# Later chunks' last two values products moved between the fourth up quarter and its rest, and a new order of the steps

## The chip, the cores and the metric

The kernel runs on one core of one Trainium2 chip. The metric is the device time in microseconds of one execution; a time is the median of the runs shown. The profile is of one execution, whose own time stands beside its span.

## The reference

Two blocks follow one another. An mLSTM cell (batch 4, 8 heads, 768 steps, head size 40) is followed by a dense layer pair with an exact gelu (3072 tokens, 320 to 2048 to 320), all in float32:

```python
for t in range(S):
    m_new = np.maximum(f_gate[:, :, t] + m, i_gate[:, :, t])
    f_stab = np.exp(f_gate[:, :, t] + m - m_new)
    i_stab = np.exp(i_gate[:, :, t] - m_new)
    C = f_stab[..., None, None] * C + i_stab[..., None, None] * np.einsum('bhd,bhe->bhde', vt, kt)
    n = f_stab[:, :, None] * n + i_stab[:, :, None] * kt
    h_tilde = np.einsum('bhde,bhe->bhd', C, qt)
    denom = np.maximum(np.abs(np.einsum('bhd,bhd->bh', n, qt)[:, :, None]), 1.0)
    y[:, :, t] = o * h_tilde / denom          # o = sigmoid(o_gate)
x = y.transpose(0, 2, 1, 3).reshape(B * S, H * D)
h = x @ w_in
out = (0.5 * h * (1.0 + erf(h / sqrt(2)))) @ w_out
```

## The kernel before

**Chunks.** The 768 steps are cut into six chunks of 128. Within a chunk the cell is written as matrix products: decayed scores of q and k (tile `W`), their product with the values (`values`, `later_values`, tile `ph`), and the part that comes from the state carried in from earlier chunks (`read_two`, tile `pf`, scaled into the tile `far`). The sum of the last two is `hs`. `finish` divides it and applies the output gate, `turn_y` transposes the result into `px`, and `split_x` makes the operands of the dense layers of it.

**Dense layers.** Each chunk has 512 tokens (4 batches of 128). Every float32 operand is split into parts of fewer bits, and three products of parts stand for one (`x_hi`, `x_rest`, `x_low`; `g_parts`; `w_out_part`). The up product is made in four quarters: `up` (line 966: 24 products with 128 rows, tile `pu`) and then `up_rest` (line 977: 12 with 64 rows). `gelu` (lines 984 to 987) takes a bank of it to `g_whole` and three parts. `down` (line 991) adds 12 products of one row block into the accumulators `po`, one bank for each batch. A bank has 512 columns and `po` uses 320; the view `beside` names 164 columns behind them.

**The order is written by hand.** Three strings of words give the order in which the steps are issued: `FRONT` for chunk 0, all gates, the weights' conversion and the cell of chunk 1; `SECOND` for the dense layers of chunk 1 beside the cell of chunk 2; `LATER` for those of chunks 2 to 4 beside the cells of 3 to 5. `LAST` (chunk 5, dense layers alone) does not change. `play` calls the step of each word. Each engine, and each queue, executes what it is given in that order; between engines there are waits on data and buffers only.

**Letters of the later chunks** (the number is the quarter, the batch or the row block): `U`/`u` up and up_rest, `g` gelu, `d` down, `E` finish of the chunk before (output copy, line 1015, and its sends, line 859, on SP's queue), `L` load of the blocks of q and k, `K`/`Q` their transposes (line 512, VectorE), `D` weighing of the values (line 539, GpSimd), `C` read_two (line 621), `h` update_two (lines 632 to 647), `S` scores_two (lines 568, 574), `V` later_values (lines 674, 678), `Y` the cell's finish (lines 685 to 690), `t` twice (line 699, ScalarE), `X` turn_y (lines 708, 718), `R` split_x (lines 727, 728), `M` mask (line 474, GpSimd), `W` exponentials (line 500), `G` gate (line 506), `B`, `J`, `O` loads, `+` one copy from DRAM to DRAM. A number of 4 or more means the next chunk's cell.

**Letters of the front** that the argument uses: `K` conv_one (lines 404, 405, ScalarE) and `J` conv_two (lines 416, 419, VectorE) convert piece after piece of the weights (tiles `sig` and `pow`, two buffers each; `J` also issues a later piece's load); `z` splits a row block of chunk 0's gelu (873, 875 on ScalarE, 874 on VectorE); `a`/`b` split rows of w_out (935, 943); `F` is one row block of chunk 0's down product (line 888), sixteen in all, the last six made of parts; `X`, `Y`, `R`, `G` belong to the cell of chunk 1; `r` and `p` send the gates out and back.

**Buffers the change touches.** The pool `outp` has two buffers with the tag `o_sb`, which hold the output until it is sent; `raw` has two with the tag `sig`, used for `g_whole` in the later chunks; `fars[0]` has two with the tag `hs`. `side` and `main` are two pairs of PSUM pools, two banks under each tag, that change places from chunk to chunk. In `later_values` the batches 0 and 1 write `beside` without starting a new sum and the batches 2 and 3 a bank of their own.

Of the kernel before, what the change touches and what calls it, by code (L numbers as in the profile page):

```python
# [9 lines left out]
F32 = mybir.dt.float32  # L10
# [4 lines left out]
OP = mybir.AluOpType  # L15

P = 128
# [6 lines left out]


FRONT = """
    O0 L0 k1 P0 E L1 L2 t0 P1 k7 K w0 g0 N s0 w1 O1 O3 D k4 t1 P2 w2 c0 v0 J y0 Q s1 L3 O2 K d w3 q t2 L4 P3 v1
    g1 c1 J y1 s2 K x0 t3 x1 v2 g2 O4 J B4 g3 c2 y2 s3 B5 K x2 K L5 J T0 K v3 A y3 M1 x3 c3 G0 M0 H O7 O6 O5 J
    J i5 u0 L6 u1 K W0 J W1 I4 A K S0 T1 C0 J i6 V0 i7 u2 G2 K U M2 L7 S1 J G1 K U i8 W2 J i9 C1 T2 K
    M3 f2 S2 V1 Y0 T3 J Y1 C2 e W3 K K K J S3 J C3 f3 K X0 J K R0 J K J V2 K Y2 J J K  # L30
    K V3 X1 J K r F J K (0 )0 F J K F K J F X2 G3 F J K F Y3 R1 J K F p + + + + J F J a10,2 b10,2 z10 a12 b12 F X3 z11 F a13,3 b13,3 z12 F z13 [1 F B8 z14 F B9 R2 z15 F R3 B10 B11 F a8 b8 a9 b9 F"""
CELL = "MWGVYXRKQDCSht"

HI_AT = {3: ("w_out3", 0), 8: ("w_out3", 2), 4: ("w_out0", 0), 5: ("w_out0", 1), 6: ("w_out2", 0), 7: ("w_out2", 1), 9: ("f0", 0)}
# [1 line left out]
for at, first, key in ((HI_AT, 10, "h0"), (LO_AT, 10, "h1"), (HI_AT, 13, "b0"), (LO_AT, 13, "b1"), (HI_AT, 0, "b2"), (LO_AT, 0, "b3")):  # L36
    at.update((first + i, (key, i)) for i in range(3))
LATER = """
 U0 u0 E0 E1 E2 E3 K1 Q1 L2 D0 D1 C0 h0 M2 M3 g0 g1 g2 g3 +
 U1 u1 g4 d0 g5 d1 g6 d2 g7 S0 d3 K2 Q2 L3 W2 W3 G0 G1 G2 G3 +  # L40
 U2 V0 V1 u2 g8 d4 g9 K3 Q3 B4 B5 J0 J1 d5 g10 d6 g11 S2 L4 d7
 U3 u3 + M4 M5 Y0 Y1 D2 D3 K4 W4 W5 g12 t0 d8 g13 t1 d9 g14 X0 X1 R0 d10 g15 R1 C2 h2 O0 O1 d11 V2 V3 Y2 t2 B6 J2 d12 Y3 t3 Q4 L5 B7 d13 X2 X3 R2 d14 R3 d15 + O2 O3"""

SECOND = """
 U0 u0 j2 o0 o1 K1 Q1 L2 M0 M1 D0 D1 W0 W1 a0,3 b0,3 a3 b3 a4,2 b4,2 a6,2 b6,2 C0 h0 M2 M3 g0 g1 g2 g3 o2 o3 + +
 U1 u1 Z Z Z g4 d0 g5 d1 g6 d2 g7 S0 d3 K2 Q2 L3 W2 W3 G0 G1 G2 G3 Z Z +
 U2 V0 V1 u2 + g8 d4 g9 K3 Q3 B4 B5 J0 J1 d5 g10 d6 g11 S2 L4 d7
 U3 u3 + M4 M5 Y0 Y1 D2 D3 K4 W4 W5 g12 t0 d8 g13 t1 d9 g14 X0 X1 R0 d10 g15 R1 C2 h2 O0 O1 d11 V2 V3 Y2 t2 B6 J2 d12 Y3 t3 Q4 L5 B7 d13 X2 X3 R2 d14 R3 d15 + O2 O3"""

LAST = """  # L50
 U0 u0 E0 E1 E2 E3 g0 g1 g2 g3 U1 u1 g4 d0 g5 d1 g6 d2 g7 d3 
# [5 lines left out]
def kernel(  # L57
# [16 lines left out]
    nc = tc.nc  # L74

    B, H, S, D = q.shape
    L = P
    NCH = S // L
    NP = H // 2
    D1 = D + 1  # L80
    DP = 64
    BH = B * H
    DM = H * D
    DFF = moe_w_in.shape[1]
    NF = DFF // P
    TG = B * L
# [13 lines left out]
    raw = ctx.enter_context(tc.tile_pool(name="raw", bufs=2))  # L100
    two = ctx.enter_context(tc.tile_pool(name="two", bufs=2))
    outp = ctx.enter_context(tc.tile_pool(name="outp", bufs=2))
    dram = ctx.enter_context(tc.tile_pool(name="dram", bufs=1, space=bass.MemoryType.DRAM))
    ps_tr = ctx.enter_context(tc.tile_pool(name="ps_tr", bufs=2, space=bass.MemoryType.PSUM))
    ps_h = ctx.enter_context(tc.tile_pool(name="ps_h", bufs=2, space=bass.MemoryType.PSUM))
    ps_mm = ctx.enter_context(tc.tile_pool(name="ps_mm", bufs=2, space=bass.MemoryType.PSUM))
# [25 lines left out]
    vb = [const.tile([P, H, D1], F32, name=f"vb{n}", tag=f"vb{n}") for n in range(NQ)]  # L132
# [63 lines left out]
    def turn_of(n):  # L196

        return n % NLD if n < 2 * B else (n - 2 * B) % NQ
# [184 lines left out]
    bits, sig, pow2 = {}, {}, {}  # L383
# [51 lines left out]
    def per_head(t, c, b):  # L435
        return t[:, c, b * H:(b + 1) * H].unsqueeze(2)
# [9 lines left out]
    def in_place(x, b):  # L446

        return x.rearrange("p k (a t) -> p (k a) t", a=2)[:, :, b * R:(b + 1) * R]
# [9 lines left out]
    class Cell:  # L458
# [153 lines left out]
        def read_two(self, b0):  # L612

            c, two_b = self.c, (b0, b0 + 1)
            banks = self.banks = [self.side[1][0].tile([P, H + NP, D1], F32, name="pf", tag=self.side[1][1]) for _ in range(2)]
            for i, b in enumerate(two_b):
                qT = self.qT[b]
                for p in range(NP):
                    for r in halves:
                        for hip in range(2):  # L620
                            nc.tensor.matmul(banks[hip][r, NP * i + p, :], qT[halves[hip], p, r],  # L621
                                             state[b][halves[hip], p, 0:D1], start=True, stop=True)

        def update_two(self, b0):

            c, two_b, banks = self.c, (b0, b0 + 1), self.banks
            if c + 1 < NCH:
                for i, b in enumerate(two_b):
                    vw = self.vw.pop(b)
                    for p in range(NP):  # L630
                        for hip in range(2):
                            nc.tensor.matmul(banks[i][used[hip], H + p, :], k_later[turn_of(c * B + b)][:, 2 * p + hip, :],  # L632
                                             vw[:, 2 * p + hip, :], start=True, stop=True)
            add = []
            for i, b in enumerate(two_b):
                self.far[b] = fars[0].tile([P, H, D1], F32, name="far", tag="hs", bufs=2)
                by_hip = lambda t, hip: t.rearrange("p (m two) d -> p m two d", two=2)[:, :, hip, :]
                for hip in range(2):
                    nc.vector.tensor_tensor(out=by_hip(self.far[b], hip), in0=banks[hip][:, NP * i:NP * i + NP, :],  # L639
                                            in1=by_hip(per_head(gT, c - 1, b), hip).to_broadcast([P, NP, D1]), op=OP.mult)  # L640
                if c + 1 < NCH:
                    st, d = state[b][:, :, 0:D1], dec[:, c - 1, b * NP:(b + 1) * NP].unsqueeze(2).to_broadcast([P, NP, D1])
                    nc.gpsimd.tensor_tensor(out=st, in0=st, in1=d, op=OP.mult)
                    for r in used:
                        add.append((st[r], banks[i][r, H:H + NP, :]))
            for st, to in add:
                nc.vector.tensor_tensor(out=st, in0=st, in1=to, op=OP.add)

# [11 lines left out]

        def later_values(self, b):

            n, hs = self.c * B + b, self.far.pop(b)
            Pm = W.pop(n)
            by_hip = lambda t: [t.rearrange("p (m two) d -> p m two d", two=2)[:, :, hip, :] for hip in range(2)]
            if b < 2:
                ph = beside[2 * b:2 * b + 2]
            else:
                whole = self.side[0][0].tile([P, H, D1], F32, name="ph", tag=self.side[0][1])
                ph = by_hip(whole)  # L670
            for hip in range(2):
                for p in range(NP):
                    for r in quarters:
                        nc.tensor.matmul(ph[hip][r, p, :], Pm[:, 2 * p + hip, r], vb[turn_of(n)][:, 2 * p + hip, :], start=b > 1,  # L674
                                         stop=True, skip_group_check=b < 2)
            self.hs[b] = hs
            for to, x in zip(by_hip(hs), ph) if b < 2 else ((hs, whole),):
                nc.vector.tensor_tensor(out=to, in0=x, in1=to, op=OP.add)

        def finish(self, b):  # L680
            n, hs = self.c * B + b, self.hs.pop(b)
# [18 lines left out]

        def turn_y(self, b):
            n, t = self.c * B + b, slice(b * L, (b + 1) * L)
            pool, tag = self.side[b // 2] if self.c > 1 else (ps_tr, "tr") if self.c > 0 else (ps_mm, "b")
            px = pool.tile([P, NX + 1, L], F32, name="px", tag=tag)
            unread(px[:, 0, :])
            for k in range(NX + 1):
                y = ob[n % NLD][:, k * P:(k + 1) * P] if k < NX else self.rest.get(b, y_rest).rearrange("p two r -> p (two r)")
                nc.tensor.transpose(px[:, k, :], y, ident)  # L708
            self.turned.append(b)
            if self.c < 2 and len(self.finished) > len(self.turned):  # L710
                self.twice(b + 1)
            if self.c == 0:
                nc.scalar.copy(out=first_x[:, :, t], in_=px)
                return
            self.px[b] = px
            if "x" not in parts:
                parts["x"] = raw.tile([P, NX + 1, TG], F32R, name="x_hi", tag="x", bufs=1)
            nc.scalar.activation(out=in_place(parts["x"], b), in_=by_set(px), func=AF.Copy, scale=PART)
            if self.c == 1 and b < 2:
                load(n + NLD, 1, 3)  # L720
# [12 lines left out]
    parts, fars, w_hi, w_lo, beside = {}, [], {}, {}, []  # L733
# [304 lines left out]
    def first_blocks():  # L1038
# [3 lines left out]
        for r in (32, 96):  # L1042
# [8 lines left out]
                 d=lambda: decays_last(0, 1), q=lambda: decays_last(1, NCH - 1), r=halves_out, p=halves_back,  # L1051
                 A=in_turn(first_up_steps(0)), U=in_turn(first_up_steps(1)), e=first_blocks, F=in_turn(first_down_steps(first_g)),
                 K=in_turn(lambda i=i: conv_one(i) for i in n_pieces), H=products_begin,
                 J=in_turn(lambda i=i: conv_two(i) for i in n_pieces), Z=split_weight,
# [53 lines left out]
```

## Time and profile before

| | us |
|---|---|
| median of 3 runs | 438.81 (438.38 to 438.86) |
| the profiled execution, own time | 438.46 |
| its span (first to last instruction) | 436.7 |
| chunk 1's dense layers | 118.85 to 184.72 of the span |
| chunk 2 / 3 / 4 | from 184.72 / 249.96 / 315.52 |
| chunk 5, end of its products | 379.39 / 433.0 |

In the rows of the profile a line has the engine (PE is TensorE, PEld its weight loads, DVE VectorE, ACT ScalarE, POOL GpSimd, SPq the queue of DMAs issued by SyncE), the line of the kernel, the operation, the tiles written and read, their shapes and a count. A timeline gives the start, the duration and, in brackets, the engine's idle time before it with what ended it. The chain of waits goes back from the last instruction, each time to what released it.

### The profile page before, as it was taken

The page shows a single profiled execution, that of the slowest core. Times are in us where ns is not written, and L with a number is a line of the kernel's source. Part 1 is how long each engine was busy: PE and PEld are TensorE (multiplying, and loading weights), DVE is VectorE, ACT ScalarE, POOL GpSimd, SP SyncE. Part 2 cuts the span into 40 slices and gives each one's busy share as a digit, 9 for nine tenths or more (in the row PEclk, how much of TensorE's full clock was granted, in tenths as well). Part 3 has the DMA queues.
Part 4 walks back from the last instruction along what each step waited for, and adds up shares of the span by engine and source line. Part 5 has one row for each costly group of instructions (what it writes and reads, how often), then busy time and mean ns, then how long its engine had stood idle before and what let it go on. Part 6 is the DMA issues. An engine that isn't in the chain of part 4 may idle for free.

```text
span 436.7 us, 13291 instructions
## 1 busy us (share of the span) xinstructions
PE 427.3 (98%) x5472; PEld 374.6 (86%) x5472; DVE 296.0 (68%) x680; ACT 277.3 (63%) x595; POOL 48.8 (11%) x77
## 2 busy tenths in 40 slices
PE   8989999999999999999999999999999999999996
PEld 7777888877988899988899988899988889979986
DVE  8797687797888697747597747597746586533330
ACT  4989999856889985228785229785247715243441
POOL 3001030000430041030041030040010000000000
PEclk9999999999999999999999999999999999999999
DMA  7999994577791592662492653571561400010001
GB/s 151 220 214 243 233 256 87 138 211 179 229 154 56 106 176 60 115 179 50 84 187 42 123 158 60 117 134 32 110 156 17 62 2 2 22 42 2 1 2 60
DMA packets 162268, 48.83 MB, mean 112 GB/s; under 512 B 147776, under 2 KB 155232, under 8 KB 162208
## 3 DMA queue, kind: packets, MB, share of 16 engines
q1 hardware_dynamic: 161888, 47.65, 50.1%
q8 instruction: 43, 0.70, 0.6%
q10 hardware_dynamic: 320, 0.33, 0.2%
q14 instruction: 17, 0.14, 0.1%
HBM read 43.84 MB, written 9.37 MB: 122 GB/s over the span
## 4 chain that ended last, share of the span: by engine, by line
PE 73%; DVE 2%; ACT 2%; DMA 1%; issue 1%; ACTq 0%
PE po L991 31%; PE pu L966 24%; PE pu L977 7%; PE ps L568 3%; PE pf L621 2%; PE ph L674 1%; PE po L888 1%; PE po L674 1%; PE px L708 1%; DMA bits<-in_moe_w_out_dram 1%; PE pf L632 1%; DVE pow L416 1%; DVE w_out L419 0%; ACT w_out_part L935 0%; ACT g_part L873 0%
## 5 line engine op out<-in xcount | busy, mean ns | idle before, releaser
L991 PE MATMUL po<-w_out_part,g_parts 128*128 128x320 f32 x960 | 140.7, 303 | 0.0
L991 PEld LDWEIGHTS po<-w_out_part,g_parts 128*128 128x128 f32 x960 | 131.6, 189 | 5.9 <-issue 4.6
L986 DVE TENSOR_TENSOR g_parts<-g_whole,g_parts 128x512 fp32r<-128x512 f32 x80 | 57.0, 713 | 58.1 <-ACT g_parts L985 56.0
L984 ACT ACTIVATE g_whole<-pu 128x512 f32<-128x512 f32 x80 | 47.1, 589 | 74.2 <-PE pu L977 63.7
L985 ACT ACTIVATE g_parts<-g_whole 128x512 fp32r<-128x512 f32 x80 | 50.5, 631 | 8.3 <-PE po L991 5.1
L474 POOL TENSOR_SCALAR_AFFINE_SELECT W<-W 128x1024 f32<-128x1024 f32 (+2 forms) x20 | 21.7, 1088 | 189.2 <-DMA W<-M_d 154.4
L500 ACT ACTIVATE W<-W,aT 128x128 f32<-128x128 f32 x128 | 38.8, 389 | 0.3
L987 DVE CAST g_parts<-g_whole 128x512 fp32r<-128x512 f32 x80 | 36.2, 453 | 0.0
L699 ACT COPY far<-ob 128x128 f32<-128x128 f32 x16 | 4.6, 290 | 32.9 <-DVE ob L690 32.9
L966 PE MATMUL pu<-x_hi,w_in_hi 128*128 128x512 f32 x80 | 24.2, 384 | 0.0
L966 PE MATMUL pu<-x_hi,hi_first 128*128 128x512 f32 x80 | 24.0, 381 | 0.1
L966 PE MATMUL pu<-x_rest,hi_first 128*128 128x512 f32 x80 | 23.8, 379 | 0.0
L966 PE MATMUL pu<-x_rest,w_in_hi 128*128 128x512 f32 x80 | 23.8, 379 | 0.0
L966 PE MATMUL pu<-x_low,w_in_lo 128*128 128x512 f32 x80 | 23.8, 379 | 0.0
L966 PE MATMUL pu<-x_low,w_in 128*128 128x512 f32 x80 | 23.8, 379 | 0.0
L888 PE MATMUL po<-w_out,g 128*128 128x320 f32 x80 | 22.0, 432 | 0.0
L404 ACT ACTIVATE sig<-bits 128x320 f32<-128x320 f32 (+1 forms) x26 | 15.2, 586 | 10.4 <-issue 6.1
L574 DVE TENSOR_TENSOR W<-ps,W 128x256 f32<-128x256 f32 (+1 forms) x48 | 17.7, 414 | 4.2 <-PE ps L568 3.2
L888 PEld LDWEIGHTS po<-w_out,g 128*128 128x128 f32 x80 | 15.0, 190 | 5.9
L639 DVE TENSOR_TENSOR far<-pf,gT 128x164 f32<-128x164 f32 x32 | 8.4, 319 | 16.1 <-PE pf L632 11.7
L416 DVE SCALAR_TENSOR_TENSOR pow<-sig,pow 128x320 uint32<-128x320 uint32 (+1 forms) x26 | 15.4, 592 | 4.3 <-ACT pow L405 4.3
L1015 ACT ACTIVATE o_sb<-po 128x320 f32<-128x320 f32 x20 | 7.5, 443 | 16.7 <-PE po L991 16.7
(196 smaller groups left out, 778.9 us busy)
## 6 DMA issues: line engine op xcount, KB each, us to landing
W<-M_d SPq DMA_DIRECT2D x16, 512.0 KB, 6.5
bits<-in_moe_w_in_dram SPq DMA_DIRECT2D x20, 256.0 KB, 4.2
bits<-in_moe_w_out_dram SPq DMA_DIRECT2D x16, 320.0 KB, 4.6
blocks<-kq_d SPq DMA_DIRECT2D x32, 128.0 KB, 3.5
ob<-in_o_gate_dram SPq DMA_DIRECT2D x24, 160.0 KB, 4.1
out_dram<-o_sb SPq DMA_DIRECT2D x36, 80.0 KB, 2.0
wide<-M_d SPq DMA_DIRECT2D x4, 512.0 KB, 4.8
kq_d<-in_k_dram SPq DMA_DIRECT2D x6, 320.0 KB, 4.6
```

The costliest lines, as they stand in the source:

```text
L416: nc.vector.scalar_tensor_tensor(out=p, in0=s, scalar=3, in1=p, op0=OP.logical_shift_left, op1=OP.bitwise_or)
L474: nc.gpsimd.affine_select(out=x, in_=x, compare_op=OP.is_ge, fill=1.0e30, base=base, pattern=[[0, H], [1, x.shape[2]]], channel_multiplier=-1)
L500: nc.scalar.activation(out=W[n][:, h, :], in_=src, func=AF.Exp, scale=-1.0, bias=aT[:, self.c, r:r + 1])
L574: nc.vector.tensor_tensor(out=w[r, :, t], in0=ps[i][hip][r, :, t], in1=w[r, :, t], op=OP.mult)
L888: nc.tensor.matmul(to, xs[k][:, b * L:(b + 1) * L], w, start=(n == 0 and k == 0), stop=(n == NF - 1 and k + 1 == len(xs)), skip_group_chec ...
L966: nc.tensor.matmul(in_pairs(pus[i][e]), w3(at[k])[n][:, e, i * P:(i + 1) * P], in_turns(x3[n][:, k, :]), start=(n == 0 and k == 0), stop=F ...
L977: nc.tensor.matmul(in_pairs(pus[i][e]), w3(r)[n][h, p % 2, i * P:(i + 1) * P], in_turns(x3[n][h, NX, :]), start=False, stop=(n == 2), skip ...
L984: nc.scalar.activation(out=whole, in_=self.pus[n // 4][n % 4 // 2][n % 2], func=AF.Gelu)
L985: nc.scalar.activation(out=hi, in_=whole, func=AF.Copy, scale=PART)
L986: nc.vector.tensor_tensor(out=rest, in0=whole, in1=hi, op=OP.subtract)
L987: nc.vector.tensor_copy(out=low, in_=whole)
L991: nc.tensor.matmul(in_pairs(self.po[t]), x[:, t * L:(t + 1) * L], in_turns(w), start=(n == 0 and k == 0), stop=(n == NF - 1 and k == 2), s ...
```

## The change

1. `later_values`: the batches 2 and 3 also use `beside`. After the batches 0 and 1 are added to their `hs`, VectorE writes zeros into the four `beside` views, and the batches 2 and 3 are summed onto them. Their result is copied into `hs` rather than added to `far`.
2. `update_two`: the `far` of batches 0 and 1 lies in an `o_sb` buffer, that of 2 and 3 in a `sig` buffer, and for 2 and 3 it is added to `hs` here.
3. `read_two` and `turn_y` exchange their PSUM pools between the two pairs of batches.
4. New orders. `LATER` and the second half of `SECOND`: `V2 V3` stand between `U3` and `u3`; `C2 h2` stand before `X0`; `X0` to `X3` stand singly. `LATER` alone: `C0` stands between `U0` and `u0`, `M3` before `D0`. `FRONT`: many steps are permuted; the words are the same.

```diff
 FRONT = """
-    g1 c1 J y1 s2 K x0 t3 x1 v2 g2 O4 J B4 g3 c2 y2 s3 B5 K x2 K L5 J T0 K v3 A y3 M1 x3 c3 G0 M0 H O7 O6 O5 J
-    J i5 u0 L6 u1 K W0 J W1 I4 A K S0 T1 C0 J i6 V0 i7 u2 G2 K U M2 L7 S1 J G1 K U i8 W2 J i9 C1 T2 K
-    M3 f2 S2 V1 Y0 T3 J Y1 C2 e W3 K K K J S3 J C3 f3 K X0 J K R0 J K J V2 K Y2 J J K
-    K V3 X1 J K r F J K (0 )0 F J K F K J F X2 G3 F J K F Y3 R1 J K F p + + + + J F J a10,2 b10,2 z10 a12 b12 F X3 z11 F a13,3 b13,3 z12 F z13 [1 F B8 z14 F B9 R2 z15 F R3 B10 B11 F a8 b8 a9 b9 F"""
+    c1 J y1 s2 K x0 t3 x1 v2 g2 c2 O4 J B4 y2 B5 s3 g3 K L5 J T0 x2 K K M1 v3 A y3 c3 M0 G0 x3 H J O6 O5 J O7 u0
+    L6 u1 K i5 W0 J W1 A K S0 C0 I4 T1 G2 J i6 u2 U i7 V0 K M2 S1 J G1 M3 L7 K U C1 i8 J W2 T2 i9 K f2 Y0 S2 V1
+    T3 J Y1 C2 K e W3 K J K S3 J C3 f3 K X0 J K J K K R0 J K V2 Y2 J J J K K V3 (0 X1 K F G3 J )0 J
+    K F J r F J F F X2 + R1 K K p F J Y3 + F + J z10 a12 K F a10,2 b10,2 J + b12 z11 F a13,3 b13,3 z12 F F X3 z13 F
+    B8 z14 F B9 R2 z15 F [1 R3 F a8 B10 B11 a9 b9 F b8"""
...
 LATER = """
- U0 u0 E0 E1 E2 E3 K1 Q1 L2 D0 D1 C0 h0 M2 M3 g0 g1 g2 g3 +
- U1 u1 g4 d0 g5 d1 g6 d2 g7 S0 d3 K2 Q2 L3 W2 W3 G0 G1 G2 G3 +
- U2 V0 V1 u2 g8 d4 g9 K3 Q3 B4 B5 J0 J1 d5 g10 d6 g11 S2 L4 d7
- U3 u3 + M4 M5 Y0 Y1 D2 D3 K4 W4 W5 g12 t0 d8 g13 t1 d9 g14 X0 X1 R0 d10 g15 R1 C2 h2 O0 O1 d11 V2 V3 Y2 t2 B6 J2 d12 Y3 t3 Q4 L5 B7 d13 X2 X3 R2 d14 R3 d15 + O2 O3"""
+ E0 U0 E1 E2 K1 Q1 E3 L2 D1 C0 M3 u0 D0 h0 g0 g1 g2 g3 M2 U1 u1 g4 + d0 d1 g5 g6 d2 g7 S0 d3 K2 Q2 L3 G2 W2 W3 G3 G1 G0
+ + U2 V0 V1 u2 d4 K3 g8 Q3 B4 B5 g9 d5 J0 J1 g10 d6 g11 S2 L4 d7 U3 M5 Y0 M4 W5 W4 t0 Y1 t1 V2 V3 K4 u3 D3 D2 g12 d8 + g13
+ d9 g14 C2 h2 X0 d10 Y2 g15 X1 t2 Y3 t3 Q4 d11 R0 R1 d12 O0 O1 X2 d13 R2 B6 J2 d14 X3 R3 L5 B7 + O2 O3 d15"""
...
         def read_two(self, b0):
-            banks = self.banks = [self.side[1][0].tile([P, H + NP, D1], F32, name="pf", tag=self.side[1][1]) for _ in range(2)]
+            pool, tag = self.side[0 if b0 else 1]
+            banks = self.banks = [pool.tile([P, H + NP, D1], F32, name="pf", tag=tag) for _ in range(2)]
...
         def update_two(self, b0):
-                self.far[b] = fars[0].tile([P, H, D1], F32, name="far", tag="hs", bufs=2)
+                self.far[b] = (raw.tile([P, TG], F32, name="far", tag="sig") if b0 else
+                               outp.tile([P, 2, DM], F32, name="far", tag="o_sb").rearrange("p two d -> p (two d)"))[:, 0:H * D1].rearrange(
+                                   "p (h d) -> p h d", d=D1)
...
+            for b in two_b if b0 else ():
+                hs = self.hs[b]
+                nc.vector.tensor_tensor(out=hs, in0=self.far.pop(b), in1=hs, op=OP.add)
             for st, to in add:
                 nc.vector.tensor_tensor(out=st, in0=st, in1=to, op=OP.add)
...
         def later_values(self, b):
-            n, hs = self.c * B + b, self.far.pop(b)
+            n = self.c * B + b
+            hs = self.hs[b] = self.far.pop(b) if b < 2 else fars[0].tile([P, H, D1], F32, name="hs", tag="hs", bufs=2)
...
+            ph = beside[b % 2 * 2:b % 2 * 2 + 2]
...
+            for to, x in zip(by_hip(hs), ph):
+                if b < 2:
+                    nc.vector.tensor_tensor(out=to, in0=x, in1=to, op=OP.add)
+                else:
+                    nc.vector.tensor_copy(out=to, in_=x)
+            if b == 1:
+                for x in beside:
+                    nc.vector.memset(x, 0.0)
...
         def turn_y(self, b):
-            pool, tag = self.side[b // 2] if self.c > 1 else (ps_tr, "tr") if self.c > 0 else (ps_mm, "b")
+            pool, tag = self.side[1 - b // 2] if self.c > 1 else (ps_tr, "tr") if self.c > 0 else (ps_mm, "b")
```

More of the change, by code (lines that the diff above doesn't have):

```diff
@@ L26 @@
 FRONT = """
-    O0 L0 k1 P0 E L1 L2 t0 P1 k7 K w0 g0 N s0 w1 O1 O3 D k4 t1 P2 w2 c0 v0 J y0 Q s1 L3 O2 K d w3 q t2 L4 P3 v1
-    g1 c1 J y1 s2 K x0 t3 x1 v2 g2 O4 J B4 g3 c2 y2 s3 B5 K x2 K L5 J T0 K v3 A y3 M1 x3 c3 G0 M0 H O7 O6 O5 J
-    J i5 u0 L6 u1 K W0 J W1 I4 A K S0 T1 C0 J i6 V0 i7 u2 G2 K U M2 L7 S1 J G1 K U i8 W2 J i9 C1 T2 K
-    M3 f2 S2 V1 Y0 T3 J Y1 C2 e W3 K K K J S3 J C3 f3 K X0 J K R0 J K J V2 K Y2 J J K
-    K V3 X1 J K r F J K (0 )0 F J K F K J F X2 G3 F J K F Y3 R1 J K F p + + + + J F J a10,2 b10,2 z10 a12 b12 F X3 z11 F a13,3 b13,3 z12 F z13 [1 F B8 z14 F B9 R2 z15 F R3 B10 B11 F a8 b8 a9 b9 F"""
+    O0 L0 k1 P0 E L1 L2 t0 P1 k7 K w0 g0 N s0 w1 O1 O3 D k4 t1 P2 w2 c0 v0 J y0 Q s1 L3 O2 K d w3 q t2 L4 P3 v1 g1
+    c1 J y1 s2 K x0 t3 x1 v2 g2 c2 O4 J B4 y2 B5 s3 g3 K L5 J T0 x2 K K M1 v3 A y3 c3 M0 G0 x3 H J O6 O5 J O7 u0
[3 more added lines that the diff above has]
+    B8 z14 F B9 R2 z15 F [1 R3 F a8 B10 B11 a9 b9 F b8"""
 CELL = "MWGVYXRKQDCSht"
@@ L38 @@
 LATER = """
- U0 u0 E0 E1 E2 E3 K1 Q1 L2 D0 D1 C0 h0 M2 M3 g0 g1 g2 g3 +
- U1 u1 g4 d0 g5 d1 g6 d2 g7 S0 d3 K2 Q2 L3 W2 W3 G0 G1 G2 G3 +
- U2 V0 V1 u2 g8 d4 g9 K3 Q3 B4 B5 J0 J1 d5 g10 d6 g11 S2 L4 d7
- U3 u3 + M4 M5 Y0 Y1 D2 D3 K4 W4 W5 g12 t0 d8 g13 t1 d9 g14 X0 X1 R0 d10 g15 R1 C2 h2 O0 O1 d11 V2 V3 Y2 t2 B6 J2 d12 Y3 t3 Q4 L5 B7 d13 X2 X3 R2 d14 R3 d15 + O2 O3"""
+ E0 U0 E1 E2 K1 Q1 E3 L2 D1 C0 M3 u0 D0 h0 g0 g1 g2 g3 M2 U1 u1 g4 + d0 d1 g5 g6 d2 g7 S0 d3 K2 Q2 L3 G2 W2 W3 G3 G1 G0
+ + U2 V0 V1 u2 d4 K3 g8 Q3 B4 B5 g9 d5 J0 J1 g10 d6 g11 S2 L4 d7 U3 M5 Y0 M4 W5 W4 t0 Y1 t1 V2 V3 K4 u3 D3 D2 g12 d8 + g13
+ d9 g14 C2 h2 X0 d10 Y2 g15 X1 t2 Y3 t3 Q4 d11 R0 R1 d12 O0 O1 X2 d13 R2 B6 J2 d14 X3 R3 L5 B7 + O2 O3 d15"""
 SECOND = """
[L45 to L48, printed above, removed]
+ U0 u0 j2 o0 o1 K1 Q1 L2 M0 M1 D0 D1 W0 W1 a0,3 b0,3 a3 b3 a4,2 b4,2 a6,2 b6,2 C0 h0 M2 M3 g0 g1 g2 g3 o2 o3 + + U1 u1 Z Z Z g4
+ d0 g5 d1 g6 d2 g7 S0 d3 K2 Q2 L3 W2 W3 G0 G1 G2 G3 Z Z + U2 V0 V1 u2 + d4 K3 g8 Q3 B4 B5 g9 d5 J0 J1 g10 d6 g11 S2 L4
+ d7 U3 M5 Y0 M4 W5 W4 t0 Y1 t1 V2 V3 K4 u3 D3 D2 g12 d8 + g13 d9 g14 C2 h2 X0 d10 Y2 g15 X1 t2 Y3 t3 Q4 d11 R0 R1 d12 O0 O1 X2
+ d13 R2 B6 J2 d14 X3 R3 L5 B7 + O2 O3 d15"""
 LAST = """
@@ L661, in later_values @@
         def later_values(self, b):
-            n, hs = self.c * B + b, self.far.pop(b)
+            n = self.c * B + b
+            hs = self.hs[b] = self.far.pop(b) if b < 2 else fars[0].tile([P, H, D1], F32, name="hs", tag="hs", bufs=2)
             Pm = W.pop(n)
             by_hip = lambda t: [t.rearrange("p (m two) d -> p m two d", two=2)[:, :, hip, :] for hip in range(2)]
[L666 to L670, printed above, removed]
+            ph = beside[b % 2 * 2:b % 2 * 2 + 2]
             for hip in range(2):
@@ L673, in later_values @@
                     for r in quarters:
[L674 to L678, printed above, removed]
+                        nc.tensor.matmul(ph[hip][r, p, :], Pm[:, 2 * p + hip, r], vb[turn_of(n)][:, 2 * p + hip, :], start=False,
+                                         stop=True, skip_group_check=True)
+            for to, x in zip(by_hip(hs), ph):
[6 more added lines that the diff above has]
+                    nc.vector.memset(x, 0.0)
         def finish(self, b):
```

## The prediction

> **What bounds the kernel now.** I read the busy shares first, then the chain of waits in order of time, then TensorE's timeline where its pieces do not join, and last the timelines of what it waits for there.
>
> ```profile
> span 436.7 us, 13291 instructions
> PE 427.3 (98%) x5472; PEld 374.6 (86%) x5472; DVE 296.0 (68%) x680; ACT 277.3 (63%) x595; POOL 48.8 (11%) x77
> ```
>
> TensorE has 9.4 us without work. So a new order can gain only what TensorE waits, or what it loses between its own steps, and it can lose any amount through a new wait. From 118.85 us on the chain of waits is TensorE's without a hole worth a line, but for one in chunk 1. Before that, the last place with waits is the end of chunk 0's down product (F11 to F16, 72 products of parts):
>
> ```profile
> 107.50 0.93 PE L888 MATMUL po<-w_out_part,g_part 128*128 128x320 f32 x4
> 108.70 3.53 PE L888 MATMUL po<-w_out_part,g_part 128*128 128x320 f32 x24 [0.27 <-DVE g_part L874]
> 112.61 6.24 PE L888 MATMUL po<-w_out_part,g_part 128*128 128x320 f32 x44 [0.38 <-DVE g_part L874]
> 118.69 0.59 PE L966 MATMUL pu<-x_hi,hi_first 128*128 128x512 f32 x2
> ```
>
> The last 44 start 0.138 us apart ((118.69 - 112.61) / 44). At that pace the first 4 would be through at 108.05 and the 24 at 112.01, so the two waits cost 0.65 and 0.60, together 1.25 us (the brackets show less, because the modelled ends overlap the wait).
>
> **Part 1, the front.** What is late there:
>
> ```profile
> 101.70 0.58 ACT L405 ACTIVATE pow<-bits,low_bits 128x320 uint32<-128x320 uint32 x1
> 105.26 0.50 ACT L404 ACTIVATE sig<-bits 128x320 f32<-128x320 f32 x1 [2.99 <-issue]
> 106.83 0.63 ACT L873 ACTIVATE g_part<-g 128x512 fp32r<-128x512 f32 x1
> 107.36 0.60 ACT L875 CAST g_part<-g 128x512 fp32r<-128x512 f32 x1
> 107.87 0.49 ACT L935 CAST w_out_part<-w_out 128x320 fp32r<-128x320 f32 x1
> 101.45 0.49 DVE L685 SCALAR_TENSOR_TENSOR ob<-ob,far 128x320 f32<-128x320 f32 x1 [0.58 <-ACT ob L506]
> 104.68 0.50 DVE L419 SCALAR_TENSOR_TENSOR w_out<-sig,pow 128x320 uint32<-128x320 uint32 x1
> 107.96 0.68 DVE L874 TENSOR_TENSOR g_part<-g,g_part 128x512 fp32r<-128x512 f32 x1
> 111.87 1.28 DVE L874 TENSOR_TENSOR g_part<-g,g_part 128x512 fp32r<-128x512 f32 x2
> ```
>
> ScalarE stands idle from 102.28 to 105.26 in front of K26. The profile names nothing, but `sig` has two buffers, and J24, which frees the one K26 needs, ends at 105.18 (104.68 + 0.50), behind Y3 and R1 on VectorE, which start at 101.45. Everything ScalarE gives TensorE at the end (a10, z10, a12, z11, a13, z12) is queued behind that idle K26. In the new order J24 comes before Y3, and z10 and a12 before K26: their 1.5 us (106.83 to 108.36) fill the hole. Even if K26 stayed at 105.26, z12 and all before it would come 1.5 us earlier on ScalarE, and the two late VectorE rows (z10's at 107.96, z12's at 111.87) would miss their dates no more: 1.5 is over 0.65 and over 0.60. X3 now follows F11, and r's two DMAs stand behind two loads of weight pieces, which come earlier for it. The other permutations leave the sums on ScalarE and VectorE before each of TensorE's steps about as they were, where TensorE has no wait to lose. I take -1.25; the bounds are 0 (another producer becomes as late) and -1.25.
>
> **Part 2, V2 and V3.** Their 128 products move; what do they cost in each place?
>
> ```profile
> 147.81 1.44 PE po L674 x118
> 175.22 1.48 PE ph L674 x120
> 176.69 0.35 issue
> 177.04 0.27 PE ph L674 x3
> 177.31 3.46 PE po L991 x24
> 181.46 3.26 PE po L991 x24
> 213.67 1.38 PE po L674 x112
> 241.02 1.51 PE ph L674 x117
> 306.59 1.50 PE ph L674 x114
> ```
>
> `po` rows are V0 V1 between U2 and u2, `ph` rows V2 V3 between two downs. 24 downs behind V3 take 3.46, behind downs 3.26: a further 0.20 for the change of form. Between an up and its rest I see no such loss. So a chunk saves 1.51 + 0.20 - 1.38 = 0.33 (chunk 2), the same in chunks 3 and 4, and 1.48 + 0.35 + 0.27 + 0.20 - 1.44 = 0.86 in chunk 1, if its hole of 0.35, unexplained, goes too. Together -1.85; bounds -0.5 (only the bare durations) and -1.85. C2 h2 before X0 instead of a down moves the 0.20, it does not remove it.
>
> VectorE gets four memsets and four copies of 164 columns and two additions of 328, and loses two additions. These touch the accumulators' banks, so d4 has to wait for the memsets and d8 for the copies:
>
> ```profile
> 149.00 1.03 DVE L678 TENSOR_TENSOR far<-po,far 128x164 f32<-128x164 f32 x4
> 150.74 5.09 PE po L991 x36
> L268 DVE MEMSET state<- 128x328 f32 x3 | 1.0, 332 | 0.1
> ```
>
> Chunk 1 is the tightest: the additions end at 150.03, d4 begins at 150.74 and reaches the fourth bank 0.41 later. A memset of twice the columns takes 332 ns; at half of that, four end at 150.7, at the full 332 ns at 151.4. I take 0; bounds 0 and 0.2 in one chunk. [...]
>
> **Part 3, a new wait.** `far` of batch 1 now takes the `o_sb` buffer from which E2 and E3 are being sent, and these sends are late on SP's queue:
>
> ```profile
> out_dram<-o_sb SPq DMA_DIRECT2D x36, 80.0 KB, 2.0
> 186.71 7.53 SPq L859 DMA_DIRECT2D out_dram<-o_sb  x8
> 252.20 8.37 SPq L859 DMA_DIRECT2D out_dram<-o_sb  x8
> 259.98 0.59 SPq L859 DMA_DIRECT2D out_dram<-o_sb  x1
> 317.18 7.15 SPq L859 DMA_DIRECT2D out_dram<-o_sb  x8
> 184.72 5.18 PE pu L966 x24
> 249.96 5.18 PE pu L966 x24
> 315.52 5.18 PE pu L966 x24
> 258.18 1.11 DVE L639 TENSOR_TENSOR far<-pf,gT 128x164 f32<-128x164 f32 x4 [5.44 <-PE pf L632]
> 259.21 1.34 DVE L647 TENSOR_TENSOR state<-state,pf 40x164 f32<-40x164 f32 x4
> 258.44 5.38 PE pu L966 x24
> ```
>
> In chunk 3 the last send is issued at 259.98 and lands 2.0 later, 12.0 after U0's start (249.96). By the same sum chunk 2's lands 10.9 and chunk 4's 10.2 after U0's start. VectorE wants the buffer 8.7 after it (258.18 + 0.5). What is queued behind: batch 1's `far` (0.5), the state's additions, whose first half (0.67) frees the first `pf` bank, then g0 to g3. U1's second half writes that bank; it begins at 258.44 + 0.2 + 12 x 0.216 = 261.2, 11.3 after U0's start (0.216 is 5.18 / 24). So U1 stands if the sends land later than 11.3 - 0.1 - 0.5 - 0.67 = 10.0. In the new tail the transpose Q4, which lets SP go on to the next loads and so to the sends, ends 0.5 earlier against U0, so I take landings at 10.4, 11.5 and 9.7: stalls of 0.4 in chunk 2, 1.5 in chunk 3, none in chunk 4, which also has no state to add. Together +1.9; bounds 0 (the sends go out at 0.6 each) and +2.9 (nothing comes earlier). Chunk 1 has no E.
>
> **Part 4, the tail.** Behind h2 VectorE now has `far`, additions, state, Y2, g15, Y3, Q4 and four R before U0 needs the last operand.
>
> ```profile
> 305.27 1.02 DVE L639 TENSOR_TENSOR far<-pf,gT 128x164 f32<-128x164 f32 x4
> 313.84 0.55 DVE L728 CAST x_low<-px 128x384 fp32r<-128x384 f32 x1
> ```
>
> Before, this stretch took 9.1 (305.27 to 314.39) and ended 1.1 before U0 at 315.52. Now it also holds g15 (1.0) and two R (1.9), less about 0.1 for the additions and the pauses: some 12 us. TensorE has from h2's middle to U0 11.65 us (X's 4 x 0.33, 0.20, six downs at 1.63, 0.35 of h2), and reaches the last x_low 0.86 later: 12.5. A margin of 0.5 to 0.8; I take 0.
>
> **The sum.** 438.46 - 1.25 - 1.85 + 1.9 = 437.26 against the profiled execution's own time, which is 0.35 under the median; against the median 437.61. I forecast 437.4.
>
> **The rivals.**
>
> Sends early. SP reaches them early enough, part 3 costs nothing: 437.4 - 1.9 = 435.5. For it: a send takes only 0.59 once they run. Against: in three chunks eight of them took 7.15 to 8.37.
>
> No gain in the front. Another wait takes the place of K26's: 437.4 + 1.25 = 438.65, no change. Against: the 1.5 us that z10 and a12 move.
>
> Sends later, the slower side. O3, just ahead of the sends on SP, waits for X3, which now comes 1.6 before U0 instead of 3.3. If the sends land 1.5 later than I take them, U1 stands 1.9, 3.0 and about 1 us: 4 us more, 441.4. It is slower than before from 0.8 us of lateness in each chunk, less than the spread between the three chunks now (10.2 to 12.0).
>
> VectorE the bound of the tail. If its operations stretch beside GpSimd's, U0 waits in four chunks for what exceeds the margin of part 4; at 1 us over, 4 us: 441.4 as well. Slower from 0.55 over.
>
> **How the numbers follow.** Forecast 0.42, sends early 0.20, front without gain 0.14, sends later 0.16, tail 0.08. Forecasting alone, 436.2 to 438.6. About 0.2% (0.9 us) is what can be told from no change: faster means under 437.9, slower over 439.7. Faster: most of the forecast's share (0.35) and the early sends (0.20), 0.55. Same: the rest of the forecast and the front without gain, with a little from the late cases, 0.22. Slower 0.23. The range for 8 in 10 leaves out the ends of both sides: 435.0 to 440.8.
>
> **What would show it.** F11 to F16 without a bracket, K26's idle time under 1 us, and U0 of chunk 1 near 117.6; V2 V3 at 1.4 with no dearer down behind; in chunks 2 and 3 VectorE idle before the second half of line 639 with a DMA `out_dram<-o_sb` as what ended it, and a hole in U1's middle (0.4, 1.5), none in chunk 4; no hole at U0. Wrong would be a hole at X1, d4, S0 or U0, or a U1 without one.

## The result: 0.5% slower, and the profile after

The changed kernel takes 439.96 us (median of 17 runs, 438.93 to 443.19), the kernel before, run beside it, 438.36 (17 runs, 436.52 to 440.08). The ratio is 1.0048, with a 95% interval of 1.0032 to 1.0064. The forecast was 437.4, with a range of 435.0 to 440.8. The time lies inside the range, but on the other side of the old one. The profiled execution took 440.24 us. Four of the 17 runs have a mean granted clock of TensorE of 0.995 or 0.996 and take 441.90 to 443.19 us; none of them left a trace, and the other 13 have a median of 439.64.

In the rows of the changed kernel the line numbers have moved: up is 974 (966 before), down 999 (991), the products of parts in the front 896 (888), `far` 642 (639), the state's additions 653 (647), the sends 867 (859). The experiments shift them by a few more.

The page of the changed kernel (its span, then busy time, share of the span and instructions of each engine):

```profile
span 438.5 us, 13282 instructions
PE 426.6 (97%) x5472; PEld 374.4 (85%) x5472; DVE 302.6 (69%) x712; ACT 278.6 (64%) x595; POOL 49.0 (11%) x77
```

TensorE's busy time fell by 0.7 us and the span grew by 1.8, so TensorE now waits 2.5 us longer. The chain of waits shows in which chunk. Here are the starts of U0 in chunks 1 to 5 and of U3 (225.57, 291.76, 357.05) in chunks 2 to 4:

```profile
118.45 5.18 PE pu L974 x24
...
183.52 5.18 PE pu L974 x24
...
225.57 5.18 PE pu L974 x24
...
250.20 5.18 PE pu L974 x24
...
291.76 5.18 PE pu L974 x24
...
316.38 5.18 PE pu L974 x24
...
357.05 5.18 PE pu L974 x24
...
381.17 5.18 PE pu L974 x24
```

The same view of the kernel before, U3 in chunks 2 to 4 and the last U0:

```profile
224.96 5.18 PE pu L966 x24
...
290.29 5.42 PE pu L966 x24
...
355.01 5.18 PE pu L966 x24
...
379.39 5.18 PE pu L966 x24
```

From U0 to U0 the chunks took 65.87, 65.24, 65.56 and 63.87 us before, and 65.07, 66.68, 66.18 and 64.79 after. From U3 to the next U0, where V2 V3 were moved, chunks 2 to 4 took 25.00, 25.23 and 24.38, and now 24.63, 24.62 and 24.12. What is left over belongs to the first part of each chunk:

| term | forecast | profiled execution | from |
|---|---|---|---|
| front, up to U0 of chunk 1 | -1.25 | -0.40 | 118.45 - 118.85 |
| chunk 1 and the tails of 2 to 4 | -1.85 | -2.04 | -0.80 - 0.37 - 0.61 - 0.26 |
| U0 to U3 of chunks 2 to 4 | +1.9 | +4.22 | (1.44 + 0.37) + (0.62 + 0.61) + (0.92 + 0.26) |
| sum | -1.2 | +1.78 | 440.24 - 438.46 |

The third line is the loss. TensorE's timeline around the middle of U1 in chunks 2, 3 and 4:

```profile
194.20 0.59 PE L974 MATMUL pu<-x_low,w_in_lo 128*128 128x512 f32 x2
196.37 0.67 PE L974 MATMUL pu<-x_hi,w_in_hi 128*128 128x512 f32 x2 [1.58 <-DVE state L653]
...
260.88 0.59 PE L974 MATMUL pu<-x_low,w_in_lo 128*128 128x512 f32 x2
262.48 0.67 PE L974 MATMUL pu<-x_hi,w_in_hi 128*128 128x512 f32 x2 [1.01 <-DVE state L653]
...
326.32 0.59 PE L974 MATMUL pu<-x_low,w_in_lo 128*128 128x512 f32 x2
327.79 0.67 PE L974 MATMUL pu<-x_hi,w_in_hi 128*128 128x512 f32 x2 [0.87 <-DVE far L642]
```

The products start 0.216 apart, so the second halves were due at 194.63, 261.31 and 326.75. They started 1.74, 1.17 and 1.04 us later, 3.95 together. VectorE's timeline says what it waited for in front of the second half of `far`:

```profile
195.09 0.56 DVE L642 TENSOR_TENSOR far<-pf,gT 128x164 f32<-128x164 f32 x2 [1.55 <-DMA out_dram<-o_sb]
...
261.20 0.56 DVE L642 TENSOR_TENSOR far<-pf,gT 128x164 f32<-128x164 f32 x2 [2.01 <-DMA out_dram<-o_sb]
...
327.31 0.56 DVE L642 TENSOR_TENSOR far<-pf,gT 128x164 f32<-128x164 f32 x2 [2.33 <-DMA out_dram<-o_sb]
```

This is the wait of the prediction's part 3, at the place it named, but in three chunks and not in two, and twice as long. The last sends stand in the chain (start and time until landing):

```profile
193.02 1.96 DMA out_dram<-o_sb
...
259.12 1.96 DMA out_dram<-o_sb
...
324.89 1.95 DMA out_dram<-o_sb
```

They land at 194.98, 261.08 and 326.84, which is 11.5, 10.9 and 10.5 us after U0. TensorE goes on 1.39, 1.40 and 0.95 later.

In the front the two waits are gone. TensorE's timeline of the 72 products has no bracket, and K26 stands on ScalarE without idle time behind z10 and a12:

```profile
107.94 2.03 PE L896 MATMUL po<-w_out_part,g_part 128*128 128x320 f32 x12
...
110.06 8.40 PE L896 MATMUL po<-w_out_part,g_part 128*128 128x320 f32 x60
```

```profile
102.03 0.48 ACT L943 CAST w_out_part<-w_out 128x320 fp32r<-128x320 f32 x1
102.42 0.49 ACT L404 ACTIVATE sig<-bits 128x320 f32<-128x320 f32 x1
```

Two questions remain. Is the wait for the sends the whole loss of the later chunks, and why did the front bring 0.40 where its waits were worth 1.25?

### The profile page after: what moved, and what is told of

Read it like the earlier page. It is cut to its first block, busy times and chain, and to the rows that moved or that the text cites. A ratio compares the mean times of both kernels' runs of the same rounds, so it can differ in the third digit from the quotient of the medians.

```text
span 438.5 us, 13282 instructions
## 1 busy us (share of the span) xinstructions
PE 426.6 (97%) x5472; PEld 374.4 (85%) x5472; DVE 302.6 (69%) x712; ACT 278.6 (64%) x595; POOL 49.0 (11%) x77
## 4 chain that ended last, share of the span: by engine, by line
PE 82%; issue 10%; ACT 3%; DMA 1%; DVE 1%; POOL 1%; SPq 0%; DVEq 0%; POOLq 0%
PE po L999 30%; PE pu L974 22%; PE po L896 7%; PE pu L985 6%; PE ps L568 3%; PE po L677 3%; PE pu L795 2%; PE pf L622 2%; PE px L716 2%; DMA out_dram<-o_sb 1%; ACT W L500 1%; PE pu L826 1%; ACT g_whole L992 1%; PE ps L552 1%; PE pu L801 1%
## 5 line engine op out<-in xcount | busy, mean ns | idle before, releaser
L994 DVE TENSOR_TENSOR g_parts<-g_whole,g_parts 128x512 fp32r<-128x512 f32 x80 | 55.4, 693 | 45.3 <-ACT g_parts L993 43.1
L995 DVE CAST g_parts<-g_whole 128x512 fp32r<-128x512 f32 x80 | 33.6, 420 | 0.0
L726 ACT ACTIVATE x_hi<-px 128x384 fp32r<-128x384 f32 x20 | 9.8, 488 | 21.0 <-PE px L716 21.0
L974 PEld LDWEIGHTS pu<-x_hi,w_in_hi 128*128 128x128 f32 x80 | 14.2, 189 | 6.8 <-issue 5.2
```

The lines of the kernel that those rows point to most:

```text
L974: nc.tensor.matmul(in_pairs(pus[i][e]), w3(at[k])[n][:, e, i * P:(i + 1) * P], in_turns(x3[n][:, k, :]), start=(n == 0 and k == 0), stop=F ...
L994: nc.vector.tensor_tensor(out=rest, in0=whole, in1=hi, op=OP.subtract)
L995: nc.vector.tensor_copy(out=low, in_=whole)
```

## The experiments

Ten kernels were run. Each was timed beside the kernel before (17 to 20 runs of it, medians 438.49 to 438.74) and ran 6 to 12 times; "profiled" is the one execution that left a trace.

**Both `far` in one buffer.** The changed kernel, with `far` of batches 0 and 1 side by side in one `o_sb` buffer, so that they no longer need the buffer from which E2 and E3 are sent.

```diff
-  self.far[b] = (raw.tile([P, TG], F32, name="far", tag="sig") if b0 else
-                 outp.tile([P, 2, DM], F32, name="far", tag="o_sb") ...
+  if not i and not b0:
+      both = outp.tile([P, 2 * H * D1], F32, name="far", tag="o_sb")
+  self.far[b] = (raw.tile([P, TG], F32, name="far", tag="sig")[:, 0:H * D1] if b0 else
+                 both[:, i * H * D1:(i + 1) * H * D1]).rearrange("p (h d) -> p h d", d=D1)
```

> The changed kernel, with `far` of batches 0 and 1 side by side in one `o_sb` buffer (328 columns each), so that VectorE waits for the sends of E0 and E1 alone and no longer for those of E2 and E3. Theory A (the wait of `far` for the last sends is the whole loss of the later chunks: holes of 1.74, 1.17 and 1.04 us in U1 of chunks 2, 3 and 4): the holes go, at most 0.2 us of each is left, and the profiled execution comes to 440.24 - 3.95 = about 436.3, 0.5% under the kernel before. Rival B (U1's second half has a second wait just behind, the additions of the state or the masks on GpSimd): the holes shrink to 0.5 to 1 us each and the time is 437.5 to 439. Rival C (the holes only move to the next place of the chunk): still about 440.

Measured: 436.63 us (6 runs), ratio 0.9948 (0.9932 to 0.9965), profiled 436.50. Theory A holds: this one edit turns the loss into a gain. VectorE's and TensorE's timelines show what is left, in chunk 2 alone:

```profile
193.30 1.03 DVE L643 TENSOR_TENSOR far<-pf,gT 128x164 f32<-128x164 f32 x4 [6.88 <-ACT g_parts L994]
```

```profile
194.26 0.59 PE L975 MATMUL pu<-x_low,w_in_lo 128*128 128x512 f32 x2
195.05 0.67 PE L975 MATMUL pu<-x_hi,w_in_hi 128*128 128x512 f32 x2 [0.20 <-DVE state L654]
```

`far` now runs in one piece, and U1's second half comes 0.36 late (195.05 - 194.26 - 0.43). The bracket names ScalarE; the chain leads from `far` back to a send that lands at 193.01, so what is left is a shorter wait for the sends.

**The buffer alone.** The kernel before, with only this of the change:

```diff
-  self.far[b] = fars[0].tile([P, H, D1], F32, name="far", tag="hs", bufs=2)
+  self.far[b] = (fars[0].tile([P, H, D1], F32, name="far", tag="hs", bufs=2) if b0 else
+                 outp.tile([P, 2, DM], F32, name="far", tag="o_sb") ...
```

> The kernel before, with one thing of the change alone: `far` of batches 0 and 1 in the `o_sb` ring; order, V2 V3 and front are those of before. Theory A: the last sends land 10.9, 12.0 and 10.2 us after U0 in chunks 2, 3 and 4, and U1's second half stands for what exceeds 9.9, 9.9 and 9.6: holes of 1.0, 2.1 and 0.6, together 3.7, so about 442.1, 0.8% over the kernel before. If the holes come from the new order of the sends and of the tail instead: under 439.2.

Measured: 444.38 us, ratio 1.0129 (1.0106 to 1.0152). The buffer by itself makes a hole of 1.76 us in chunk 2 and one of 2.53 in chunk 3, counted from the date at which the next product was due. TensorE's timeline in chunk 3:

```profile
261.91 0.59 PE L968 MATMUL pu<-x_low,w_in_lo 128*128 128x512 f32 x2
264.87 0.67 PE L968 MATMUL pu<-x_hi,w_in_hi 128*128 128x512 f32 x2 [2.36 <-DVE state L649]
```

Neither the order nor the place of V2 V3 is needed for the loss. Chunk 4 has no hole here, where 0.6 was expected. The time is 2.3 over the expectation, and the stretches around chunk 3's hole show most of it (busy time of each engine, then TensorE's granted clock, of which 1.00 is full speed, the DMA engines' share and GB/s):

```profile
262.00:264.80 2.80, 0.51 (x3) 0.10 (x1) 1.16 (x5) 0.00 (x0) 0.36 (x1) 1.00 0.60 114
264.80:268.80 4.00, 3.93 (x11) 3.21 (x12) 3.51 (x8) 2.17 (x4) 0.00 (x0) 0.59 0.76 132
```

Behind the hole TensorE has a granted clock of 0.59 for 4 us; by estimate that costs another 1.6 us (0.41 of 4).

**The sends first.** The changed kernel as it is, but one copy of keys and two loads of output gates stand behind the sends on SP, not ahead of them.

```diff
- E0 U0 E1 E2 K1 Q1 E3 L2 ...
+ E0 U0 E1 E2 K1 Q1 E3 + O-2 O-1 L2 ...
...
- X3 R3 L5 B7 + O2 O3 d15
+ X3 R3 L5 B7 d15
```

> The changed kernel, its buffers as they are, with one copy of keys and the two output gates' loads that stand ahead of the sends on SP moved behind them (O2 O3 of a chunk run as the next chunk's first loads). They take 1.9 us of SP's queue. If the sends follow them: landings 1.9 us earlier, 9.7, 9.1 and 8.7 us after U0, holes under 0.2 and about 436.6. If the first send's 2.6 us of waiting on SP only grows by what was moved (the queue behind it has to drain to the same date): landings and holes nearly as they are, 439.5 to 440.2.

Measured: 435.82 us, ratio 0.9938 (0.9914 to 0.9962), profiled 435.62. U1 has no hole in any chunk. The sum of the prediction without the cost of part 3, its rival "sends early", is 435.5. SP's timeline in chunk 2:

```profile
182.61 0.69 SPq L210 DMA_DIRECT2D wide<-M_d  x1
183.40 5.04 SPq L867 DMA_DIRECT2D out_dram<-o_sb  x8
188.48 0.63 SPq L182 DMA_DIRECT2D kq_d<-in_k_dram  x1
```

In the changed kernel:

```profile
185.45 8.15 SPq L867 DMA_DIRECT2D out_dram<-o_sb  x8
```

The first of these eight held SP for 2.6 us. Now they take 5.04 together, the first one no longer waits on SP, and they are through 5.4 us after U0's start (188.44 - 183.07 on the chain) where it was 10.1 (193.60 - 183.52), so 4.7 us earlier and not 1.9. So the 2.6 us for which the first send held SP belonged to the transfers ahead of it; 1.9 was the smaller part of their price.

**Three words of the front.** The kernel before, with J24 ahead of Y3 and with z10 and a12 ahead of K26, the edit that the prediction's part 1 made responsible:

```diff
- F Y3 R1 J K F p + + + + J F J a10,2 b10,2 z10 a12 b12 F
+ F J Y3 R1 z10 a12 K F p + + + + J F J a10,2 b10,2 b12 F
```

> The kernel before, with three words of the front moved: J24 ahead of Y3, z10 and a12 ahead of K26. My recorded step: TensorE's two waits of 0.65 and 0.60 in F11 to F13 go, U0 of chunk 1 starts at 118.85 - 1.25 = 117.6, the time is about 437.2. Rival (another producer is as late): U0 at 118.4 to 118.85 and 438 to 438.5.

Measured: 436.90 us (12 runs), ratio 0.9964 (0.9953 to 0.9976). TensorE's timeline has 72 products in a row, and the chain has U0 at the forecast 117.6. That it falls so near is partly luck, as the first part of this execution happened to be as early as in the profile of before (see below):

```profile
107.43 10.18 PE L891 MATMUL po<-w_out_part,g_part 128*128 128x320 f32 x72
```

```profile
117.62 5.18 PE pu L969 x24
```

**Where the front's win went.** Two kernels: the kernel before with the whole new front, and the kernel before with its own front up to S1 and the new order from there on.

> The kernel before with the whole front of the changed kernel and nothing else of it. If the 0.79 us lost ahead of 60 us belongs to that order: W0 on ScalarE at 46.5 again (45.7 to 46.6 in four executions with the order of before), U0 of chunk 1 at 118.3, time 0.4 under the kernel before, 438.1. If it was the execution's: U0 at 117.6 and 437.2.

> The kernel before, with its own front up to S1 (55 us) and the changed kernel's order of the rest. In the changed kernel TensorE is 0.79 us late at 60 us and has won 1.19 us between there and U0 of chunk 1. If the 0.79 comes from the order of the words ahead of S1 (the masks' loads and what ScalarE has to do ahead of W0): U0 of chunk 1 at about 117.65, the time about 437.3. If the win hangs on the early lateness: U0 at 118.3 or later and 437.9 or more.

Measured: 437.83 us (0.9979, 0.9965 to 0.9994) and 437.60 (0.9976, 0.9961 to 0.9991). Both expectations missed. The new front alone had U0 at 117.21 on TensorE's timeline, and the split one, with the old order in its first part, at 118.31. The timelines of all twelve traces show why. The first product of f2 (the first row `pu<-first_x_hi,hi_first`, an up product of chunk 0) falls at 62.70 to 64.09 with the new order of the first part (six executions, mean 63.5) and at 62.94 to 64.47 with the old one (six, mean 63.4). This is the spread of executions and not the order. From there to U0 it is 55.70 and 55.36 us with the old front, and 54.51 to 54.55 in all ten executions in which z10 and a12 stand ahead of K26.

**V2 V3 back.** The kernel with both `far` in one buffer, and V2 V3 taken out of U3 and put between two downs again, just before C2; then the same with one down between them and C2.

```diff
- Y1 t1 V2 V3 K4 u3 D3 D2 g12 d8 + g13 d9 g14 C2 h2
+ Y1 t1 K4 u3 D3 D2 g12 d8 + g13 d9 g14 V2 V3 C2 h2
...
+ Y1 t1 K4 u3 D3 D2 g12 d8 V2 V3 + g13 d9 g14 C2 h2
```

> The changed kernel with both `far` in one `o_sb` buffer, and V2 V3 put back between two downs, just before C2, in the zeroed columns as they are. My recorded part 2: every chunk gets dearer by 0.33 (products 1.51 for 1.38, and 0.20 for one more change of form), four chunks 1.3 together, with chunk 1's hole of 0.35 up to 1.85: 437.8 to 438.4. Rival (the place of V2 V3 is worth nothing, the loss of the holes explains all): 436.3 to 436.8.

> As values_back, but V2 V3 one down earlier, between d8 and d9, so that 12 long products stand between their 128 short ones and the 96 of C2 and h2. In values_back TensorE stood 1.46, 1.89 and 2.06 us inside C2 or h2 with nothing that the profile names, each time until 2.3 to 2.7 us after a 16 KB load of instructions began, and its granted clock was 0.62 behind the hole of 1.89. Theory F (224 short products in a row outrun TensorE's instructions): holes under 0.6 us each, no lower clock behind them, and then the place of V2 V3 alone is left, 0.33 a chunk: 436.5 + 1.3 = 437.8, with the change of form behind V3 nearer 437.3. If the hole is C2's own (a bank or an operand that it waits for, whatever stands ahead): again over 440.

Measured: 442.46 us (ratio 1.0084, 1.0053 to 1.0114) and 439.47 (12 runs; 1.0010, 0.9992 to 1.0028), against 436.63 with V2 V3 in U3. Just before C2 they cost 5.8 us. TensorE's timeline in chunk 3, the view of the DMA queues from 299 to 304 us (its first row has 40 slices of 0.125 us), and the stretch behind:

```profile
301.32 0.90 PE L622 MATMUL pf<-state,qT 64*64 64x41 f32 x47
303.89 0.45 PE L622 MATMUL pf<-state,qT 64*64 64x41 f32 x17 [1.67 <-issue]
```

```profile
DMA  0000000000000000000040000000000000000000
...
q8 instruction: 1, 0.02, 1.2%
```

```profile
304.00:308.00 4.00, 4.00 (x61) 3.88 (x61) 3.13 (x10) 1.64 (x3) 0.46 (x1) 0.62 0.25 45
```

TensorE stops inside C2, and the profile names no engine for it. The one transfer of these 5 us is a 16 KB load of instructions that begins in the slice from 301.50 on; TensorE goes on about 2.3 us after that. With 12 long products ahead of C2 the holes are gone but for one of 0.35 in chunk 4, and no lower clock follows (behind that one 12 products of down take 1.63 us on the chain, as in the other chunks, and the execution's mean granted clock is 0.999, against 0.991 with V2 V3 just before C2). So theory F stands as far as these runs go, though the time misses its 437.8. The rest of the price is mostly in the tails, 0.35, 0.63, 0.73 and 0.6 us dearer than with V2 V3 in U3, and not 0.33 each: 2.3 of the 2.77 us between the two profiled executions. TensorE's timeline shows part of it:

```profile
299.67 0.80 PE L678 MATMUL po<-vb,wide 128*32 128x41 f32 x64
300.65 2.19 PE L1000 MATMUL po<-w_out_part,g_parts 128*128 128x320 f32 x12 [0.17 <-DVE hs L684]
```

The down behind V3 waits for the copies out of its own banks, and its 12 products take 2.19 where 12 behind a transpose take 1.88.

**Together.** Both `far` in one buffer with the three words, and the sends first with the three words, each on the old front.

> The changed kernel with both `far` in one `o_sb` buffer, and with the front of the kernel before in which only J24, z10 and a12 are moved. If the two are independent: U0 of chunk 1 at 117.45 as with the three words alone (0.88 earlier than with both `far` in one buffer, 118.33), the chunks as there, so the profiled execution 436.5 - 0.9 = 435.6, 0.7% under the kernel before. If the later chunks give it back (a tail or a queue that was hidden by the later start): 436.2 or more.

> The kernel with the sends first, and with the front of before in which only J24, z10 and a12 are moved. With the whole new front U0 of chunk 1 started at 117.21, 117.83, 117.91, 118.29 and 118.33 in five executions, with the three words at 117.45 and 118.98, with the front of before at 118.68 and 118.69. If the fronts are equal within the spread of executions: 435.8 within 0.6. If the three words alone are the better front: 435.2 or less.

Measured: 436.27 us (0.9947, 0.9926 to 0.9968) and 435.84 (0.9938, 0.9920 to 0.9955). The fronts are equal within the spread. The first of the two falls into its second branch, 436.2 or more, and its profiled execution (437.42) had f2 at 64.47, the latest of the twelve, so this run doesn't tell the branches apart. The changed kernel with its sends first, 435.82 and 435.84, is 0.6% faster than the kernel before.

## Why the prediction was wrong

**Bound.** Right: what was lost shows as TensorE waiting, and no other engine became the bound of a chunk.

**Part 1, the front.** The cause was right, and the size nearly so. With J24, z10 and a12 alone the two waits are gone, and the stretch from f2 to U0 is 1.15 to 1.19 us shorter than in the profile of before in each execution that has the move; against the other trace with the old front it is 0.85 at most. The profile of the change showed only 0.40, because its first part happened to be 0.79 later (63.78 against 62.99), which is inside the 1.8 us over which the twelve executions spread there. One profiled execution can't resolve a term of 1 us behind a stretch that varies by more.

**Part 2, V2 V3.** Right within 0.2: -2.04 for -1.85. Some 0.24 of it is luck: in chunk 3 of the profile of before U3 took 5.42 us, where three of the other four traces with that order have 5.18. Chunk 1 gained 0.80 for 0.86. What the prediction called an unexplained hole of 0.35 resembles those of the experiment with V2 V3 before C2: it ends 2.4 us after a 16 KB load of instructions begins (177.04 - 174.67). Of the other four traces with V2 V3 in the old place, two have such a hole at V3's last products (0.42 and 0.27 by the brackets) and two have none. The rival that VectorE bounds the tail fell: no hole at U0 in any chunk. Stretching as it names it shows in the trace of before: one VectorE operation of line 986 took 1.58 us with GpSimd's mask beside it (line 474, 221.27 to 222.47), where the median of the 80 is 0.69. Only X1 of chunk 4 started 0.23 late. The chain leads from it to ScalarE's `g_whole`, which stood 0.52 until VectorE had added `far` to `hs` (line 651): the `far` in the `sig` buffer is a second, small wait that the prediction didn't have. The memsets (195 ns each) cost nothing, as taken: the profile has d4's weight loads released by them, 0.33 us by the bracket in each of the four chunks, but the kernel before has the same 0.33 there without a memset (`issue`), and in chunk 1 d4 begins 0.31 behind u2's last pair of products in both (150.30 - 149.99, 150.67 - 150.36).

**Part 3, the failing step.** The wait is the one foreseen, but its cost was forecast at 1.9 us and measured at 3.95: "In the new tail the transpose Q4, which lets SP go on to the next loads and so to the sends, ends 0.5 earlier against U0, so I take landings at 10.4, 11.5 and 9.7: stalls of 0.4 in chunk 2, 1.5 in chunk 3, none in chunk 4, which also has no state to add." The landings were 11.5, 10.9 and 10.5: later than before in chunks 2 and 4 and earlier in chunk 3 alone. Q4 did end 0.5 earlier, and SP began the loads behind it 0.47 earlier against U0. SP's timeline in chunk 2, the kernel before and then the changed one:

```profile
181.39 2.46 SPq L191 DMA_DIRECT2D blocks<-kq_d  x4
...
179.72 2.71 SPq L191 DMA_DIRECT2D blocks<-kq_d  x4
```

But the queue doesn't keep that lead. In chunk 2 the first send began 1.93 us after U0 where it had been 1.99, and the eight took 8.15 where they had taken 7.53. In chunk 3 it began 1.85 after U0 (2.24 before), in chunk 4 2.29 (1.66 before). The sends wait on SP for the transfers ahead of them (sends_first); what sets the date at which these are done was not tested.

Also, the limit of 10.0 was too late. By the stalls it is 9.7 in chunks 2 and 3 (11.46 - 1.74 and 10.88 - 1.17): U1's second half was due 11.1 after U0 (194.63 - 183.52) and not 11.3, and the release through `far` and the state's additions took 1.4 and not 1.27. In chunk 4 it is 9.4 (10.46 - 1.04), because U1 stands 0.74 earlier there already in the old profile (323.26 - 315.52 against 258.44 - 249.96), which I had not counted. Of the 2.05 us that the stalls exceed the forecast, the landings make 0.9 and the limits 1.15.

The recorded rival "sends later", which got a chance of 0.16, comes near in size: it named 1.9, 3.0 and about 1 us, and 1.74, 1.17 and 1.04 came. Its mechanism isn't in the trace. The loads of the output gates, which were to wait for X3, begin 0.2 to 1.2 us after U0, directly behind the issue ahead of them and 1.8 to 2.8 us after X3; and in chunk 3 the sends landed 0.6 earlier than I took them.

**The sum.** With the terms as measured, -2.04 + 4.22 and the front's mean over executions, -1.0 (54.52 for the mean of 55.70 and 55.36), the change costs 1.2 us. The medians say 1.6, and 1.3 with the 439.64 above; the ratio's interval is 1.4 to 2.8, so a part of the loss over all runs is in none of these terms.

## What to carry to other kernels

When a tile is put into a buffer that is being sent from, set the landing of the last send against the date at which the new writer, and what is queued behind it, is needed: here the writer waited 1.55, 2.01 and 2.33 us by the brackets, and U1 stood 3.95 in three chunks. The landings moved by 0.2 to 1.1 us against U0 from one order to the other, in both directions, so a margin of 1 us on such a queue wasn't one: move the sends ahead of what is not urgent, or use the buffer that was sent first. And before one profiled execution is used to price an early stretch, look how far that stretch varies from execution to execution.

## What the runs showed of the hardware

**Behind three holes TensorE's granted clock fell.** Behind holes of 1.67, 1.84 and 2.36 us by the profile's brackets (two with V2 V3 before C2, one with the buffer alone), the granted clock was 0.62, 0.71 and 0.59 over the next 4 us; behind the five of 0.87 to 1.59, three of them the changed kernel's, it stayed at 1.00. Behind the hole of 2.36 products of U1 start 0.43 us apart ((268.62 - 266.06) / 6), and 0.216 otherwise. What parts the hole of 1.67 from that of 1.59 isn't shown.

**TensorE stood inside a long row of short products.** With 128 products of 41 columns and the 96 of C2 and h2 right behind them TensorE stood 1.46, 1.89 and 2.06 us, each time until 2.3 to 2.7 us after a 16 KB load of instructions began. With one down of 12 long products between them, one hole of 0.35 was left. That the short products outran their instructions (theory F) is argued from this, as the profile names no wait. An estimate fits it: the pages of before and after each have 43 loads on the queue q8 (0.70 MB) and 10,944 products and weight loads of TensorE, about 254 to a load if all these loads are TensorE's, which the pages don't say; and 224 products with their weight loads are 448 instructions in a row.
